# Window attention and a token/channel mixer on one core: the second half of a weight conversion put behind the split of x, and four edits to the first tiles

## The chip, the core and the metric

The kernel runs on one core of one Trainium2 chip. A core has five engines that each work through a queue of their own in program order and wait for each other by semaphores: PE multiplies matrices (its weight loads are listed apart, as PEld), DVE (VectorE) and ACT (ScalarE) do elementwise work, POOL (GpSimd) does elementwise work on SBUF alone, SP (SyncE) issues the DMA transfers. PE writes its results to PSUM, which this kernel lays out as eight banks of 128 x 512 f32 (`s`, `pt` and `h` two each, `av` and `up` one each); DVE and ACT read them from there.

The metric is the time of one execution on the device in microseconds (us). Three runs of the kernel before took 844.10, 844.76 and 845.11 us; the median is 844.76 us.

## The reference, cut to what matters

```
# q, k, v: (8, 8, 576, 64) f32; batch 8, 8 heads, 576 positions, 64 wide
scores = q @ k.T / sqrt(64);  mask = (0 <= i - j) & (i - j < 64)     # the last 64 positions
attn   = softmax(where(mask, scores, -1e9)) @ v
x      = attn, heads side by side: (8, 576, 512)
h = relu(x.T @ w_tok1) @ w_tok2                 # over positions: 576 -> 256 -> 576
u = x + h.T
h2 = relu(u @ w_ch1) @ w_ch2                    # over channels: 512 -> 1536 -> 512
out = u + h2                                    # f32
```

The four weight matrices come as 64-bit floats. The kernel gets their words as integers and turns them into f32 itself.

## The kernel before, in words

**Three stages.** The first, up to about 262 us of the profiled execution, is attention with the token mixer and most of the weight conversion. The second and third are the channel mixer: first three chunks of 512 tokens with plain products, while the weights are rewritten for a scheme of seven products per 2 x 2 block, then six chunks with that scheme. The change touches the first stage alone.

**Tiles.** Attention is cut into 36 tiles (`i` = 0 to 35), nine for each pair of batches. A tile holds two blocks of 64 query rows, one under the other in the 128 partitions, and all eight heads. Each block needs 128 keys. The tiles with `i % 9 == 4` hold the last block of both batches of a pair, and their x is split half by half (L345 to L349).

**Steps of one tile**, with the names that the profile shows:

- `qk` (L260): 32 small products give the scores `s`, in two PSUM banks (`u` = 0 and 1). In the first seven tiles (`N_PE`) the mask is first put into the bank by a product of `identr` and `maskr` (L270), and in the later ones DVE adds it.
- `softmax` (L280): the first seven tiles take the maximum from the bank (`nm`, L290, L291). Later ones scale and mask on DVE (`e`, L293) and take the maximum from there (`nm`, L296).
- `softmax_exp` (L298): eight exponentials on ACT, four for each bank, with their sums.
- `pt_transpose` (L307): PE transposes e into `pp` (L311), ACT copies it to `pt` (L313).
- `av` (L318): 32 products of pt and v give `xp` (L323). `recip` makes `ri` of the sums (L331, L332), `norm` multiplies: `x` = xp times ri (L337), on DVE.
- `split_x` (L342): ACT rounds x to `xhi` (L101), POOL takes the rest `xlo` (L104). With both, products in the fast format keep the precision.
- `tok1` (L439, products `h` at L368), `finish_h` (`hhi` on ACT, `hlo` on DVE, L388), `tok2` (a piece: transposes of x into a bank `up` at L409, six products at L416, a copy `u` on ACT at L421) are the token mixer. Pieces run one after the exponentials of the first bank and one at the end of a tile. All use one bank, so each waits for the copy of the one before.

**Conversion.** 28 jobs turn 320 or 384 columns of 64-bit weights into f32 during this stage, one each in most tiles (table `JOBS`: tiles up to 5, 12, and from 7 on those with `i % 9` other than 0, 3 and 5). A job has three parts:

- the first half, `job_convert_a`: three tensor_scalar operations `c` on DVE (L195, L197, L198);
- the second half, `job_convert_b`: `c` (L207), `r` (L209), `r` (L210) on DVE, then the sum `w` on POOL (L212);
- the finish, `job_finish`: ACT rounds w to `t1hi`, `t2hi` or `w1hi` (L101); the rest, `t1lo` or `w1lo`, is taken by POOL and `t2lo` by DVE (both L104). Jobs 0 to 3 make t1, 4 to 6 make t2, 7 to 22 make w1, the others go to memory.

**What sets the order.** Nothing is scheduled by a planner: each engine's queue is the order in which the loop at L478 writes the steps. Iteration `i` does the transposes and the product with v of tile i, the softmax of tile i + 1 and the scores of tile i + 2. On DVE an iteration is: maximum of the first bank, ri, the first half of a job, maximum of the second bank, the second half of the job, x of tile i, then hlo where a batch is finished. The first three tiles put their x into the next iteration (`N_EARLY`, L499, L535). The finish of a job stands ahead of the exponentials of the next iteration, but in iterations 4 and 5 behind them (L503, L526). `tok1_plan` (L472) says in which iteration tok1 takes which tile. Before, iteration 4 takes tiles 2 and 3, and iteration 5 takes tile 4.

The loads at the start are written out (L458 to L471), all on SP's queue.

Of the kernel before, what the change touches and what calls it, by code (L numbers as in the profile page):

```python
# [10 lines left out]
F32 = mybir.dt.float32  # L11
# [11 lines left out]
P = 128  # L23
# [22 lines left out]
TOK1_FROM, TOK1_SLOW, TOK2_FROM = 2, 4, 7  # L46

N_PE, N_EARLY = 7, 4

# [34 lines left out]
def mixer_kernel(ctx: ExitStack, tc: tile.TileContext, qh, kh, vh, wt1, wt2, wc1, wc2, out):  # L84
# [38 lines left out]
    with ExitStack() as actx:  # L123
# [28 lines left out]
        swapped = pa.tile([P, P], F32, name="swapped")  # L152
        make_identity(nc, ident)
        nc.scalar.copy(identr, ident)
        for m in (1, 0):
# [66 lines left out]
        def job_load():  # L222
            if to_load:
                n = to_load.pop(0)
                src, _, _, o, m = jobs[n]
                raw = cpool[0].tile([P, CW], I64, name=f"raw{n}", tag="raw", bufs=3)
                nc.sync.dma_start(raw[:, :m], src[:, o:o + m])
                to_convert.append((n, raw))
# [15 lines left out]
        def job_finish():  # L244
            if to_finish:
                n, w = to_finish.pop(0)
                finished.add(n)
                src, hi, lo, o, m = jobs[n]
                if hi is None:
                    nc.sync.dma_start(w2_dram[:, o:o + m], w)  # L250
                else:
                    eng = nc.vector if src is wt2 or n >= N_FIRST else nc.gpsimd
                    split(nc.scalar, eng, hi[:, o:o + m], lo[:, o:o + m], w)
                    if src is wt1 and o + m == 5 * DT:
                        for c, r in enumerate((top, bottom)):
                            nc.gpsimd.tensor_copy(t1z[r, c], t1lo[r, 4 * DT:].bitcast(F32))
# [3 lines left out]
        def qk(i):  # L260

            qt, on_pe = loaded[i][0], i < N_PE
            s = []
            for u in range(2):
                tag, bufs = ("up", 1) if on_pe and (2 * i + u) % 3 == 2 else ("s", 2)
                s.append(ps.tile([P, 4, P], F32, name=f"s{i}_{u}", tag=tag, bufs=bufs))
                s_ps[i, u] = s[u]
                if on_pe:
                    mk = maskr[1 if tile_blocks(i)[0][1] == 0 else 0]
                    nc.tensor.matmul(s[u], identr, mk.unsqueeze(1).to_broadcast([P, 4, P]), start=True, stop=False,  # L270
                                     skip_group_check=True)
            for j in range(4):
                for u in range(2):
                    r = slice(u * BLK, (u + 1) * BLK)
                    for half, (b, n) in enumerate(tile_blocks(i)):
                        nc.tensor.matmul(s[u][half * BLK:(half + 1) * BLK, j], qt[r, j, half],  # L276
                                         kbs[b][r, j, n * BLK:n * BLK + P],
                                         start=not on_pe, stop=True, skip_group_check=on_pe)
# [184 lines left out]
        job_load()  # L463
        load_q(1)
        load_v(0)
        for g in range(2):
            nc.sync.dma_start(k0[:, :, g, P:], kh0[:, :, g, P:])
        nc.sync.dma_start(kbs[0][:, :, 8 * BLK:], kh[0, :, :, 8 * BLK:])
        load_q(2)
        job_load()  # L470
# [7 lines left out]
        for i in range(-1, NT + 1):  # L478
# [44 lines left out]
                    job_convert_a()  # L523
            if i < N_PE - 1:
                softmax_exp(i + 1, 1)
                while to_finish:  # L526
                    job_finish()
# [4 lines left out]
            for _ in range(n_jobs):  # L532
                job_convert_b()
            if 0 <= i < NT:
                xp = av(i, pts)  # L535
                if i + 1 < N_EARLY:
# [6 lines left out]
            for n in tok1_plan.get(i + 1, ()):  # L543
                if n not in xhl:
                    split_x(n)
            run_pieces(min(have, n_pieces[1]))
            while to_load and len(to_convert) < 2 and i < NT - 2:
                job_load()
# [404 lines left out]
```

## Time and profile before

The profiled execution took 845.16 us, 0.40 us more than the median of the three runs. Its span, from the first instruction to the last, is 843.4 us; the other 1.76 us lie around it.

| | busy in the span | share |
|---|---|---|
| PE | 816.6 us | 97% |
| PEld | 678.4 us | 80% |
| DVE | 528.9 us | 63% |
| ACT | 336.8 us | 40% |
| POOL | 104.8 us | 12% |

The shares are means over stages that are unlike each other. In the stretch from 62 to 262 us DVE is busy for 178.45 us of 200, ACT for 166.63; after it DVE is busy for half of the time. PE's share hides the opposite: nearly all of its idle time lies in the first stage. A wait listed for an engine costs time only where that engine is late for the one that ends last, so the rows of PE are read first.

### The profile page before, as it was taken

To read this page: it belongs to the slowest core of one execution; us is meant where nothing else is said; L and a number is where in the kernel's file an instruction comes from. 1 tells how busy PE (TensorE), PEld (TensorE's weight loads), DVE (VectorE), ACT (ScalarE), POOL (GpSimd) and SP (SyncE) were. 2 spreads that over 40 slices of the span, in tenths; PEclk is the share of its full clock that TensorE was granted. 3 is DMA by queue.
4 is the path that set the end of the run, shared out by engine and by line. 5 is a ranking of instruction groups with operands and counts; after the bars stand their busy time and mean duration, and the time that the engine had idled before them with its cause. 6 is when DMAs were issued, how large, how long until landed. Compare 5 with 4: busy or idle time off the path is not lost.

```text
span 843.4 us, 14803 instructions
## 1 busy us (share of the span) xinstructions
PE 816.6 (97%) x5864; PEld 678.4 (80%) x5864; DVE 528.9 (63%) x939; ACT 336.8 (40%) x1017; POOL 104.8 (12%) x110
## 2 busy tenths in 40 slices
PE   6889999999999999999999999999999999999998
PEld 4668888888879878888888888888888878888886
DVE  4979988888884696566425535366635367625252
ACT  4778889898885341223203211124202033202020
POOL 3533444343332000000000000000000000000000
PEclk9999999999999999999999999999999999999999
DMA  9657687676644545745412652424542325542002
GB/s 320 218 184 245 209 249 255 216 256 235 220 134 151 166 149 166 225 128 149 131 82 93 245 211 87 138 88 137 187 187 88 137 88 167 169 176 88 1 0 100
DMA packets 71621, 136.49 MB, mean 162 GB/s; under 512 B 7040, under 2 KB 41856, under 8 KB 69632
## 3 DMA queue, kind: packets, MB, share of 16 engines
q1 hardware_dynamic: 69440, 133.71, 47.0%
q10 hardware_dynamic: 2112, 1.84, 0.7%
q8 instruction: 46, 0.75, 0.4%
q14 instruction: 23, 0.19, 0.1%
HBM read 104.66 MB, written 30.87 MB: 161 GB/s over the span
## 4 chain that ended last, share of the span: by engine, by line
PE 69%; DVE 23%; ACT 3%; issue 3%; DMA 1%; POOLq 0%; SPq 0%; POOL 0%; DVEq 0%; ACTq 0%
PE gp L852 18%; PE op L640 11%; PE gp L632 8%; PE op_4a L640 4%; PE op_2b L640 4%; PE op_2a L640 4%; PE op_0b L640 4%; PE op_0a L640 4%; PE op_4b L640 4%; DVE nm L296 3%; DVE e L293 2%; PE up L416 2%; DVE x L337 2%; PE h L368 2%; DVE r L210 2%
## 5 line engine op out<-in xcount | busy, mean ns | idle before, releaser
L852 PE MATMUL gp<-m,w1hi 128*128 128x512 f32 x504 | 155.4, 390 | 0.7 <-DVE x L860 0.7
L852 PEld LDWEIGHTS gp<-m,w1hi 128*128 128x128 f32 x504 | 94.5, 188 | 21.1 <-DVE x L860 1.5
L852 PE MATMUL gp<-m,w1lo 128*128 128x512 f32 x252 | 98.0, 389 | 0.0
L304 ACT ACTIVATE e<-e,nm 128x128 f32<-128x128 f32 x232 | 90.6, 398 | 18.2 <-DVE nm L296 17.6
L619 ACT ACTIVATE ghi<-x 128x512 fp32r<-128x512 f32 x54 | 34.1, 632 | 119.9 <-DVE x L862 68.2
L856 ACT COPY x<-gp 128x512 f32<-128x512 f32 x18 | 10.4, 579 | 143.3 <-PE gp L852 143.3
L620 DVE SCALAR_TENSOR_TENSOR glo<-x,ghi 128x512 fp32r<-128x512 f32 x54 | 37.4, 693 | 38.1 <-ACT ghi L619 38.1
L619 ACT ACTIVATE ghi<-gp 128x512 fp32r<-128x512 f32 x50 | 29.9, 597 | 69.6 <-PE gp L632 69.6
L632 PE MATMUL gp<-ulo,w1hi 128*128 128x512 f32 x144 | 56.0, 389 | 0.0
L632 PE MATMUL gp<-uhi,w1hi 128*128 128x512 f32 x144 | 56.0, 389 | 0.0
L632 PE MATMUL gp<-uhi,w1lo 128*128 128x512 f32 x144 | 56.0, 389 | 0.0
L852 PEld LDWEIGHTS gp<-m,w1lo 128*128 128x128 f32 x252 | 47.3, 188 | 9.9
L620 DVE SCALAR_TENSOR_TENSOR glo<-gp,ghi 128x512 fp32r<-128x512 f32 x50 | 34.4, 688 | 25.3 <-ACT ghi L619 25.2
L640 PE MATMUL op<-glo,w2hi 128*128 128x512 f32 x128 | 49.8, 389 | 0.0
L640 PE MATMUL op<-ghi,w2hi 128*128 128x512 f32 x128 | 49.8, 389 | 0.0
L640 PE MATMUL op<-ghi,w2lo 128*128 128x512 f32 x128 | 49.8, 389 | 0.0
L323 PEld LDWEIGHTS xp<-v,pt 128*64 128x64 f32 x1152 | 37.4, 140 | 14.1 <-issue 6.5
L104 POOL TENSOR_TENSOR xlo<-x,xhi 128x512 fp32r<-128x512 f32 x32 | 41.3, 1290 | 40.3 <-ACT xhi L101 39.9
L304 ACT ACTIVATION_READ_ACCUMULATOR e<-e,nm 128x1 f32 x232 | 45.1, 194 | 0.0
L276 PE MATMUL s<-k,q 64*64 64x128 f32 x1152 | 43.0, 284 | 1.2 <-DMA k<-kh 1.2
L323 PE MATMUL xp<-v,pt 128*64 128x64 f32 x1152 | 42.3, 227 | 1.1 <-ACT pt L313 0.8
L416 PE MATMUL up<-t2hi,hhi 128*128 128x320 f32 (+1 forms) x128 | 43.0, 336 | 0.0
(165 smaller groups left out, 1881.8 us busy)
## 6 DMA issues: line engine op xcount, KB each, us to landing
v<-vh SPq DMA_DIRECT2D x36, 512.0 KB, 3.9
w1hi<-w1s SPq DMA_DIRECT2D x18, 896.0 KB, 4.8
w1lo<-w1s SPq DMA_DIRECT2D x18, 896.0 KB, 6.5
raw<-wc SPq DMA_DIRECT2D x32, 384.0 KB, 4.4
q<-qh SPq DMA_DIRECT2D x36, 256.0 KB, 4.5
k<-kh SPq DMA_DIRECT2D x7, 1280.0 KB, 8.0
out<-uf SPq DMA_DIRECT2D x35, 256.0 KB, 2.7
uf<-u_dram SPq DMA_DIRECT2D x8, 1024.0 KB, 9.5
```

Source lines behind the costliest of these rows:

```text
L104: eng_lo.tensor_sub(lo, src, hi.bitcast(F32))
L210: nc.vector.scalar_tensor_tensor(out=rf, in0=low.bitcast(U32), scalar=2.0 ** -52, in1=rf, op0=ALU.mult, op1=ALU.mult)
L276: nc.tensor.matmul(s[u][half * BLK:(half + 1) * BLK, j], qt[r, j, half], kbs[b][r, j, n * BLK:n * BLK + P], start=not on_pe, stop=True, sk ...
L296: nc.vector.tensor_reduce(out=nmu, in_=e, axis=AX.X, op=ALU.max, negate=True)
L304: nc.scalar.activation(e[:, h], src[:, h], AF.Exp, bias=nm[:, g:g + 1], scale=by, accum_out=sm[:, g:g + 1])
L323: nc.tensor.matmul(xp[half * BLK:(half + 1) * BLK, h], pts[h % 2][:, h // 2, half * BLK:(half + 1) * BLK], vt[:, half, h], start=True, sto ...
L416: nc.tensor.matmul(up[:, :n], hx[:, cs], w[:, tt * S + s0:tt * S + s0 + n], start=False, stop=(k == 6), skip_group_check=True)
L619: nc.scalar.activation(hi, src, AF.Relu)
L620: nc.vector.scalar_tensor_tensor(out=lo, in0=src, scalar=0.0, in1=hi.bitcast(F32), op0=ALU.max, op1=ALU.subtract)
L632: nc.tensor.matmul(gp, w[:, w1_at(ft, ct)], x[:, ct], start=(k == 0), stop=(k == 3 * NCT - 1))
L640: nc.tensor.matmul(op, w[:, ct, ft], x[:, cols], start=(first and k == 0), stop=(last and k == 3 * len(gs) - 1), skip_group_check=not (fir ...
L852: nc.tensor.matmul(b, w[:, at], c[:, h, t], start=(n < 4 and k == 0), stop=(k == 5), skip_group_check=True)
```

## The change

Five edits, all in the first stage.

1. **Second half of a conversion.** From iteration 4 on, `job_convert_b` stands behind av, norm, hlo, the scores of tile i + 2 and the split of x, where it stood ahead of av. The finishes that iterations 4 and 5 have at their own place move along with it. In iterations below 4 the second half stays where it was.
2. **Plan of tok1.** `TOK1_SLOW` is 5: iteration 4 takes tile 2 alone, iteration 5 takes tiles 3 and 4. From iteration 6 on the plan is the same.
3. **Products of zeros.** DVE sets a tile of 128 x 256 f32 to zero at the start, and PE multiplies it with itself, four times ahead of the first mask and three times between the masks of tile 0 and its scores. Nothing reads the result.
4. **Banks of the scores.** Tile 1 uses the two banks `h`, which are free until tok1 starts. Tiles 2 to 6 use the bank `up` at another place in their turn, and the second half of tile 7 uses it too.
5. **Loads.** q of tile 1 and the rest of the first eight blocks of k go ahead of the first weights and of v of tile 0.

```
--- before.py
+++ after.py
@@ -43,7 +43,7 @@
 JOBS = {i: 1 if i < 6 or i == 12 or i > 6 and i % TPP not in (0, 3, 5) else 0 for i in range(-1, 37)}
 PIECES = {22: (1, 0), 23: (1, 0), 31: (1, 0), 32: (1, 0), 33: (1, 0), 34: (1, 0), 35: (3, 0), 36: (2, 1)}
 
-TOK1_FROM, TOK1_SLOW, TOK2_FROM = 2, 4, 7
+TOK1_FROM, TOK1_SLOW, TOK2_FROM = 2, 5, 7
 
 N_PE, N_EARLY = 7, 4
 
@@ -150,6 +150,15 @@
         maskr = [pa.tile([P, P], F32R, name=f"maskr{m}") for m in range(2)]
         identr = pa.tile([P, P], F32R, name="identr")
         swapped = pa.tile([P, P], F32, name="swapped")
+
+        zero = pa.tile([P, 256], F32, name="zero")
+        nc.vector.memset(zero, 0.0)
+        idle = ps.tile([P, 256], F32, name="idle", tag="av", bufs=1)
+
+        def warm(k):
+            for _ in range(k):
+                nc.tensor.matmul(idle, zero[:, :P], zero, start=True, stop=True)
+
         make_identity(nc, ident)
         nc.scalar.copy(identr, ident)
         for m in (1, 0):
@@ -262,13 +271,23 @@
             qt, on_pe = loaded[i][0], i < N_PE
             s = []
             for u in range(2):
-                tag, bufs = ("up", 1) if on_pe and (2 * i + u) % 3 == 2 else ("s", 2)
+
+                if i == 1:
+                    tag, bufs = "h", 2
+                elif (i, u) == (N_PE, 1) or 2 <= i < N_PE and (2 * i + u) % 3 == 0:
+                    tag, bufs = "up", 1
+                else:
+                    tag, bufs = "s", 2
                 s.append(ps.tile([P, 4, P], F32, name=f"s{i}_{u}", tag=tag, bufs=bufs))
                 s_ps[i, u] = s[u]
+                if i == 0 and u == 0:
+                    warm(4)
                 if on_pe:
                     mk = maskr[1 if tile_blocks(i)[0][1] == 0 else 0]
                     nc.tensor.matmul(s[u], identr, mk.unsqueeze(1).to_broadcast([P, 4, P]), start=True, stop=False,
                                      skip_group_check=True)
+            if i == 0:
+                warm(3)
             for j in range(4):
                 for u in range(2):
                     r = slice(u * BLK, (u + 1) * BLK)
@@ -460,11 +479,11 @@
         k0, kh0 = (x[:, :, :8 * BLK].rearrange("p j (g n) -> p j g n", g=2) for x in (kbs[0], kh[0]))
         for g in range(2):
             nc.sync.dma_start(k0[:, :, g, :P], kh0[:, :, g, :P])
-        job_load()
         load_q(1)
-        load_v(0)
         for g in range(2):
             nc.sync.dma_start(k0[:, :, g, P:], kh0[:, :, g, P:])
+        job_load()
+        load_v(0)
         nc.sync.dma_start(kbs[0][:, :, 8 * BLK:], kh[0, :, :, 8 * BLK:])
         load_q(2)
         job_load()
@@ -523,14 +542,13 @@
                     job_convert_a()
             if i < N_PE - 1:
                 softmax_exp(i + 1, 1)
-                while to_finish:
-                    job_finish()
             for n in tok1_plan.get(i, ()):
                 tok1(n)
             if N_PE - 1 <= i < NT - 1:
                 softmax_exp(i + 1, 1)
-            for _ in range(n_jobs):
-                job_convert_b()
+            if i < 4:
+                for _ in range(n_jobs):
+                    job_convert_b()
             if 0 <= i < NT:
                 xp = av(i, pts)
                 if i + 1 < N_EARLY:
@@ -543,6 +561,12 @@
             for n in tok1_plan.get(i + 1, ()):
                 if n not in xhl:
                     split_x(n)
+            if i >= 4:
+                if i < N_PE - 1:
+                    while to_finish:
+                        job_finish()
+                for _ in range(n_jobs):
+                    job_convert_b()
             run_pieces(min(have, n_pieces[1]))
             while to_load and len(to_convert) < 2 and i < NT - 2:
                 job_load()
```

**How it moves the instructions.** The first place is SP's queue at the start. It issues the loads of q, k, v and of the first weights (raw0) in this order before:

```order
L142 DMA q0_139<-qh 128x512
L462 DMA k0_138<-kh 128x4x128 x2
L227 DMA raw0_143<-wt1 128x320
L142 DMA q1_145<-qh 128x512
L147 DMA v0_147<-vh 128x1024
L467 DMA k0_138<-kh 128x4x128 x2
L468 DMA k0_138<-kh 128x4x128
```

and in this order with the change:

```order
L142 DMA q0_142<-qh 128x512
L481 DMA k0_141<-kh 128x4x128 x2
L142 DMA q1_146<-qh 128x512
L484 DMA k0_141<-kh 128x4x128 x2
L236 DMA raw0_150<-wt1 128x320
L147 DMA v0_152<-vh 128x1024
L487 DMA k0_141<-kh 128x4x128
```

Three issues, q1 and two of k, now stand ahead of raw0, and two of k ahead of v0.

The second place is DVE's queue around x of tile 24, in a run of three tiles with jobs (19 and 20 are the jobs, L207 to L210 the second half). Before:

```order
L296 TENSOR_REDUCE nm25_2946<-e25_1_2973 128x4
L207 SCALAR_TENSOR_TENSOR c19_2969<-raw19_2600,c19_2969 128x384
L209 TENSOR_SCALAR r19_2992<-c19_2969 128x384
L210 SCALAR_TENSOR_TENSOR r19_2992<-raw19_2600,r19_2992 128x384
L337 TENSOR_TENSOR x24_3015<-xp24_2998,ri24_2951 128x512
L293 SCALAR_TENSOR_TENSOR e26_0_3071<-s26_0_3017,mask0_90 128x512
L296 TENSOR_REDUCE nm26_3069<-e26_0_3071 128x4
L331 TENSOR_SCALAR ri25_3074<-sum25_2947 128x8
```

With the change (L356 is the line of x, L216 to L219 are the second half):

```order
L315 TENSOR_REDUCE nm25_2956<-e25_1_2983 128x4
L356 TENSOR_TENSOR x24_3019<-xp24_3002,ri24_2961 128x512
L216 SCALAR_TENSOR_TENSOR c19_2979<-raw19_2610,c19_2979 128x384
L218 TENSOR_SCALAR r19_3043<-c19_2979 128x384
L219 SCALAR_TENSOR_TENSOR r19_3043<-raw19_2610,r19_3043 128x384
L312 SCALAR_TENSOR_TENSOR e26_0_3081<-s26_0_3021,mask0_90 128x512
L315 TENSOR_REDUCE nm26_3079<-e26_0_3081 128x4
L350 TENSOR_SCALAR ri25_3084<-sum25_2957 128x8
```

x and the second half change places; the scaling of the next tile (e26_0) still follows both.

The third place is POOL's queue in the same tiles. Before:

```order
L104 TENSOR_TENSOR xlo24_3036<-x24_3015,xhi24_3035 128x512
L104 TENSOR_TENSOR w1lo_67<-w19_2993,w1hi_66 128x384
L212 TENSOR_TENSOR w20_3111<-r20_3110,c20_3093 128x384
L104 TENSOR_TENSOR xlo25_3154<-x25_3133,xhi25_3153 128x512
L104 TENSOR_TENSOR w1lo_67<-w20_3111,w1hi_66 128x384
```

With the change:

```order
L221 TENSOR_TENSOR w19_3044<-r19_3043,c19_2979 128x384
L104 TENSOR_TENSOR w1lo_67<-w19_3044,w1hi_66 128x384
L104 TENSOR_TENSOR xlo25_3158<-x25_3137,xhi25_3157 128x512
L221 TENSOR_TENSOR w20_3162<-r20_3161,c20_3103 128x384
L104 TENSOR_TENSOR w1lo_67<-w20_3162,w1hi_66 128x384
```

The order per job was w, xlo, w1lo and is now xlo, w, w1lo.

More of the change, by code (lines that the diff above doesn't have):

```diff
@@ L152, in mixer_kernel, with warm @@
         swapped = pa.tile([P, P], F32, name="swapped")
+        zero = pa.tile([P, 256], F32, name="zero")
+        nc.vector.memset(zero, 0.0)
+        idle = ps.tile([P, 256], F32, name="idle", tag="av", bufs=1)
+        def warm(k):
+            for _ in range(k):
+                nc.tensor.matmul(idle, zero[:, :P], zero, start=True, stop=True)
         make_identity(nc, ident)
@@ L264, in qk @@
             for u in range(2):
-                tag, bufs = ("up", 1) if on_pe and (2 * i + u) % 3 == 2 else ("s", 2)
+                if i == 1:
+                    tag, bufs = "h", 2
+                elif (i, u) == (N_PE, 1) or 2 <= i < N_PE and (2 * i + u) % 3 == 0:
+                    tag, bufs = "up", 1
+                else:
+                    tag, bufs = "s", 2
                 s.append(ps.tile([P, 4, P], F32, name=f"s{i}_{u}", tag=tag, bufs=bufs))
                 s_ps[i, u] = s[u]
+                if i == 0 and u == 0:
+                    warm(4)
                 if on_pe:
@@ L531, in mixer_kernel @@
                 softmax_exp(i + 1, 1)
-            for _ in range(n_jobs):
-                job_convert_b()
+            if i < 4:
+                for _ in range(n_jobs):
+                    job_convert_b()
             if 0 <= i < NT:
@@ L545, in mixer_kernel @@
                     split_x(n)
+            if i >= 4:
+                if i < N_PE - 1:
+                    while to_finish:
+                        job_finish()
+                for _ in range(n_jobs):
+                    job_convert_b()
             run_pieces(min(have, n_pieces[1]))
```

10 lines of the change are left out of this document (5 added, 5 removed).

## The prediction

> **What bounds the kernel now.** First the page's chain of waits, then the busy time by stage.
>
> ```profile
> PE 69%; DVE 23%; ACT 3%; issue 3%; DMA 1%; POOLq 0%; SPq 0%; POOL 0%; DVEq 0%; ACTq 0%
> ```
> ```profile
> 0.00:62.00 62.00, 47.43 (x630) 34.82 (x631) 45.24 (x102) 41.18 (x163) 24.23 (x40) 0.97 0.70 240
> 62.00:262.00 200.00, 193.39 (x2665) 166.35 (x2663) 178.45 (x336) 166.63 (x621) 80.29 (x70) 1.00 0.66 219
> 262.00:843.40 581.40, 575.74 (x2573) 477.18 (x2572) 305.24 (x502) 129.03 (x234) 0.23 (x1) 1.00 0.39 134
> ```
>
> The columns are the stretch, its length, then PE, PEld, DVE, ACT and POOL busy. The chain gives DVE 23%, some 194 us, but PE is idle for only 14.6 us before 62, 6.6 us from there to 262 and 5.7 us after. PE and DVE are both nearly full in the attention, so the chain may follow either. PE's work stays the same, bar the zeros; what the change can win is those first two idle shares, 21 us at most. PE's longest wait from 62 to 262 says who causes most of the second one (total, times, longest):
>
> ```profile
> PE up L409 <- ACT u L421: 4.9, 7, 1.1
> ```
>
> DVE has little room either, and part of its busy time is standing. The groups of that stretch and some rows of its timeline:
>
> ```profile
> L331 DVE TENSOR_SCALAR ri<-sum 128x8 f32<-128x8 f32 x29 | 21.4, 736 | 0.0
> L197 DVE TENSOR_SCALAR c<-c 128x384 f32<-128x384 f32 x21 | 12.4, 588 | 0.7
> L198 DVE TENSOR_SCALAR c<-c 128x384 int32<-128x384 int32 x21 | 9.7, 460 | 0.7
> ```
> ```profile
> 180.23 0.16 DVE L331 TENSOR_SCALAR ri<-sum 128x8 f32<-128x8 f32 x1
> 180.55 1.25 DVE L195 TENSOR_SCALAR c<-raw 128x384 int32<-128x384 int32 x1
> 181.83 0.36 DVE L197 TENSOR_SCALAR c<-c 128x384 f32<-128x384 f32 x1
> ...
> 180.28 1.30 POOL L104 TENSOR_TENSOR xlo<-x,xhi 128x512 fp32r<-128x512 f32 x1 [3.37 <-ACT xhi L101]
> ```
>
> L195, started 0.27 us behind POOL's xlo, ends 0.22 us behind xlo's end (181.58); ri takes 0.16 us and L197 0.36 us where POOL rests, and L198 has L197's shape. So a tensor_scalar on DVE stands until POOL's operation is done. By the groups this costs 29 x (736 - 160) ns = 16.7 us at ri, 21 x (588 - 360) = 4.8 at L197 and 21 x (460 - 360) = 2.1 at L198. So the question of edit 1 is which of POOL's operations meet which of DVE's.
>
> **Start: loads, zeros, banks.**
>
> ```profile
> 2.57 0.62 SPq L227 DMA_DIRECT2D raw<-wt  x1
> 4.18 1.62 SPq L467 DMA_DIRECT2D k<-kh  x2
> 6.56 1.98 PE L276 MATMUL s<-k,q 64*64 64x128 f32 x30 [0.95 <-DMA k<-kh]
> 10.16 0.32 DVE L195 TENSOR_SCALAR c<-raw 128x320 int32<-128x320 int32 x1
> 11.12 0.79 PE L270 MATMUL s<-maskr,identr 128*128 128x512 f32 x1 [1.85 <-ACT e L304]
> 12.13 0.49 DVE L210 SCALAR_TENSOR_TENSOR r<-raw,r 128x320 f32<-128x320 uint32 x1
> 12.31 1.58 PEld L276 LDWEIGHTS s<-k,q 64*64 64x64 f32 x30 [0.19 <-DMA k<-kh]
> 14.32 0.69 DVE L290 TENSOR_REDUCE nm<-s 128x4 f32<-128x512 f32 x1 [1.70 <-PE s L276]
> 19.82 0.69 DVE L290 TENSOR_REDUCE nm<-s 128x4 f32<-128x512 f32 x1 [0.42 <-PE s L276]
> ```
>
> DVE waits at 14.32 for tile 1's scores, which wait for a bank (11.12) and for k (12.31). Now the bank is free and k goes ahead. Sizes by the shapes: 768 KB were needed at 6.56 and 2368 KB at 12.31, so 3.6 us per 1000 KB. q1 and k stand at 1536 KB, about 9.3 us; scores at the slow 2.4 us end by 11.8. raw0 stands at 1856 KB, 10.5 us. Job 0 takes DVE 2.46 us (10.16 to 12.62), so nm(1) starts at 12.9 instead of 14.32, and the 0.42 at 19.82 goes too: **1.8 us**. Bounds: 2.1 if raw0 is there at 10.16 as before, 0.1 if it takes as long from its issue as 2.57 to 10.16 (then 12.2). v of tile 0 now stands at 2368 KB, 12.3 us; its first use is behind tile 1's scores, tile 0's transposes and two ACT copies, so it is not late. The zeros hide under the wait for k that ends at 6.56. Their price is not shown; the nearest rows are the plain f32 products at 6.56, 66 ns for 128 columns on a quarter of the array. For 256 columns that is 0.13 us each if these ran one by one, 0.53 if four ran side by side: 0.9 to 3.7 us for seven. I take the upper end, for the matrix here is four times as large. From DVE's zero at about 1 us, four end near 3.1, the masks (1.22 us before) near 4.7, three near 6.3: under the wait for k, nothing. Anything beyond delays the scores one for one. Scores at a faster clock than the 1.98 us are worth nothing either: nm of tile 0 is done by 10.2 as it is, and DVE then waits for raw0 at 10.5.
>
> **Tiles 4 and 5.**
>
> ```profile
> 44.37 0.56 DVE L104 TENSOR_TENSOR t2lo<-w,t2hi 128x384 fp32r<-128x384 f32 x1 [1.79 <-ACT t2hi L101]
> 49.35 1.33 DVE L197 TENSOR_SCALAR c<-c 128x384 f32<-128x384 f32 x1
> 52.73 0.56 DVE L104 TENSOR_TENSOR t2lo<-w,t2hi 128x384 fp32r<-128x384 f32 x1 [1.66 <-ACT t2hi L101]
> 56.46 0.68 DVE L293 SCALAR_TENSOR_TENSOR e<-s,mask 128x512 f32<-128x512 f32 x1
> ```
>
> On the way to e of tile 7, at 56.46, DVE stands for 1.79 + 1.66 us behind t2hi, and for 0.97 us of L197's 1.33: 4.4 us. With the finish behind x and its split, the first t2lo waits for xhi, xlo and t2hi on ACT, about 1.8 again; the second for 0.7, since hlo (1.2 us) covers ACT's xhi; the meeting at 49.35 goes, as xlo of tile 4 is done a tile half earlier, with 0.3 for another. That leaves 2.8: **1.4 us** won after rounding down. Bounds: 0 if the waits only change their names, 3.4 if both t2lo waits vanish. Queued behind each t2lo on DVE is the second half and then the next maximum, on which ACT's exponentials wait. The plan of tok1 takes six products out of PE's wait for x of tile 3 and costs nothing elsewhere, as PE idles in tile 5. The other banks cost nothing: `h` is free until tok1 starts, and the first piece that wants `up` comes an iteration after DVE has read tile 7 from it. In tiles 3 to 6 the second bank still waits for exponentials of the same iteration, as before.
>
> **Edit 1 in the full tiles.** A tile in a run with jobs:
>
> ```profile
> 187.26 0.81 DVE L331 TENSOR_SCALAR ri<-sum 128x8 f32<-128x8 f32 x1
> 188.60 1.21 POOL L104 TENSOR_TENSOR w1lo<-w,w1hi 128x384 fp32r<-128x384 f32 x1 [0.55 <-ACT w1hi L101]
> 188.97 1.05 DVE L198 TENSOR_SCALAR c<-c 128x384 int32<-128x384 int32 x1
> 189.63 1.15 PE L323 MATMUL xp<-v,pt 128*64 128x64 f32 x32
> 190.66 0.69 DVE L296 TENSOR_REDUCE nm<-e 128x4 f32<-128x512 f32 x1
> 191.44 0.40 ACT L304 ACTIVATE e<-e,nm 128x128 f32<-128x128 f32 x1 [1.12 <-DVE nm L296]
> 192.79 0.68 DVE L337 TENSOR_TENSOR x<-xp,ri 128x512 f32<-128x512 f32 x1
> 192.95 1.01 POOL L212 TENSOR_TENSOR w<-r,c 128x384 f32<-128x384 f32 x1 [3.14 <-DVE r L210]
> 193.51 0.62 ACT L101 CAST xhi<-x 128x512 fp32r<-128x512 f32 x1 [0.41 <-DVE x L337]
> 194.20 1.29 POOL L104 TENSOR_TENSOR xlo<-x,xhi 128x512 fp32r<-128x512 f32 x1 [0.24 <-ACT xhi L101]
> 194.45 0.55 PE L409 MATMUL up<-ident,x 128*128 128x128 f32 x3 [0.67 <-ACT u L421]
> ```
>
> *Gain.* PE's 0.67 waits for u, u for xhi, xhi for x, x for the second half. Let X be the end of nm, 191.35. x now runs at X, and xhi follows the four exponentials (to X + 1.65) instead of x at X + 2.1, so u is some 0.5 to 0.6 us earlier. Over the seven gaps (4.9 us) that is up to 3.9; I take **3.0** (0 to 4.9), since a later DVE takes some back.
>
> *Cost.* xlo runs from X + 2.4 to 3.7 and now w comes right behind, to X + 4.8; w1hi and w1lo follow w. On DVE ri is due at X + 3.45 and stands 0.3 (was 0.65). L195 then meets w, 0.8 new. L198 may meet w1lo as before, 0.7: counted from w's end, it is due at 0.22 + 0.03 + 0.39 = 0.64, and w1lo after ACT's w1hi (0.53) and two hand-overs, 0.6 to 0.7. A tile costs 1.1 or 1.8; before, 0.65 or 1.35, and by the groups about 1.2 in the ten tiles that follow a job tile and have a w1lo. At even odds 0.2 each, **+2.0** (bounds -1 and +6). Third, x now waits for xp where PE is the later one, and the second half behind it waits too. Tile 10 shows it:
>
> ```profile
> 86.12 0.69 DVE L296 TENSOR_REDUCE nm<-e 128x4 f32<-128x512 f32 x1
> ...
> 86.31 1.15 PE L323 MATMUL xp<-v,pt 128*64 128x64 f32 x32
> ```
>
> nm ends at 86.81, xp at 87.46: 0.65 us that the second half (1.5 us) covered. In a full run it is the other way round (xp, 1.15 us from 189.63, ends at 190.78; X is 191.35). Nine job tiles begin a run: 0 to 5.9 us. DVE, being late, closes the gap itself, so I take **+1.0**. Behind 262 nothing moves.
>
> The page "SBUF — State Buffer" of the Trainium skill (section "Who interferes with whom") says that whoever of the two engines starts first holds a port pair for its whole instruction; the rows at 180.55 agree. It adds that a DVE operation with two SBUF inputs meets a reading GpSimd operation as well. L207 and L210 are such, and no row of this trace has them beside POOL.
>
> **Sum.** -1.8 - 1.4 - 3.0 + 2.0 + 1.0 = -3.2 us: the profiled 845.16 becomes 842.0, and 0.40 lower against the median of the runs, **841.6 us**.
>
> **Rivals.**
>
> - *Slower: w1lo wins.* It is ahead of L198 at 0.64 us from w's end in every tile: +5.6, the wait for xp 1.8, nothing won at u, the start's -3.2: +4.2, 849.0 us. For it: in the rows at 188.60 and 188.97 a w1lo that arrives under L197 goes ahead of L198. Against: the two are level by the rows. Chance 0.20.
> - *No change.* raw0 is as late as its issue (0.1 won), tiles 4 and 5 keep their waits, and 3.0 against 3.0 in the full tiles: 844.7 us. For it: DMAs in the first 12 us land together. Chance 0.22.
> - *More: both shares.* L198 always wins (-1.5 in place of +2.0), all seven gaps close (4.9), no wait for xp, capped by PE's 6.6 idle at about 5; with 3.2 from the start 836.6 us. Chance 0.15.
> - *The second half meets xlo.* Where x waits for xp by about 1.5 us, as in the lone job tiles 22 and 31, xlo starts under L207 to L210. If L210 stands for xlo's 1.29 us in two such tiles, the sum is -0.6: 844.2 us. For it: L210 reads two tensors of SBUF, as POOL's operation does. Against: nothing shows that such operations stand. Chance 0.05. By the Trainium skill's rule on two inputs (same page and section) it would come.
>
> **Numbers.** The forecast has 0.38, with 840 to 843 as its own range. The bound for a difference that a measurement of this kernel can tell is 0.2%, 1.7 us. Faster: 0.38 and 0.15, 0.53; same: the second and fourth rival with little else, 0.25; slower: 0.22. The range of 837 to 848 leaves out about half of the first rival and half of the third.
>
> **What would show it.** nm(1) near 12.9 us and the first L195 near 10.5; e of tile 7 near 53.3 instead of 56.46; from there PE's wait for u under 2 us; ri near 0.45 us mean, L195 near 0.8; L198's mean tells the first rival (0.8) from the third (0.36). If DVE's busy time from the tile at 60 us on grows by more than 5 us, or PE's idle time after 62 us rises, the sum is wrong at edit 1.

## The result

The changed kernel takes 859.67 us (median of 4 runs, 859.09 to 861.05), the kernel before 844.73: a ratio of 1.0183, with a 95% interval of 1.0171 to 1.0195. It is 15 us slower. The forecast was 841.6 us with a range up to 848, so it was wrong in sign and in size.

The profiled execution of the changed kernel has a span of 857.3 us, 13.9 us more than before. The stretch from x of tile 6 to the first product of the channel mixer holds all of it, and more (same columns as in the prediction's table by stage; first the kernel before, then the changed one):

```profile
59.97:273.31 213.34, 206.65 (x2786) 178.87 (x2787) 184.27 (x344) 175.30 (x644) 80.53 (x70) 1.00 0.66 217
```
```profile
57.60:287.73 230.13, 216.19 (x2752) 182.67 (x2751) 189.84 (x345) 174.53 (x644) 81.64 (x70) 0.99 0.60 200
```

It starts 2.4 us earlier and lasts 16.8 us longer. PE's idle time there goes from 6.7 to 13.9 us. Its busy time grows by 9.5 us, though the work is the same. A part of that is the clock: in the changed kernel the granted clock is 0.63 from 60 to 64 us, 0.68 from 280 to 284 and 0.89 from 284 to 288, together 3.2 us less than a full clock gives, where before it is full in the whole stretch. The rest is put down here to short gaps, which can count as busy since the ends of products are modelled. The waits of the weight loads show more of them. Of before, and of the changed kernel, from 58 to 290 us (total, times, longest):

```profile
PEld up L409 <- ACT u L421: 7.4, 10, 1.4
...
PEld pp L311 <- ACT e L304: 2.0, 9, 0.3
```
```profile
PEld up L428 <- ACT u L440: 10.4, 16, 2.3
PEld pp L330 <- ACT e L323: 7.7, 22, 1.5
PEld s L295 <- DVE e L312: 5.2, 10, 0.8
```

PE now waits for exponentials (7.7 us, was 2.0) and for score banks that DVE has not read yet (5.2 us; no such row before). ACT's waits from 58 to 275 us say why the exponentials are late. Before, and in the changed kernel:

```profile
ACT e L304 <- DVE nm L296: 17.6, 17, 1.4
ACT xhi L101 <- DVE x L337: 7.4, 18, 0.5
```
```profile
ACT e L323 <- DVE nm L315: 18.8, 21, 1.5
ACT w1hi L101 <- POOL w L221: 16.9, 16, 2.4
ACT xhi L101 <- DVE x L356: 4.0, 4, 3.1
```

The second row of the changed kernel is new: w1hi waits for w in each of its 16 jobs, 16.9 us in all. One tile's rows, first of before, then of the changed kernel:

```profile
159.31 1.00 POOL L212 TENSOR_TENSOR w<-r,c 128x384 f32<-128x384 f32 x1 [3.53 <-DVE r L210]
...
160.46 0.69 DVE L296 TENSOR_REDUCE nm<-e 128x4 f32<-128x512 f32 x1
...
160.56 1.29 POOL L104 TENSOR_TENSOR xlo<-x,xhi 128x512 fp32r<-128x512 f32 x1 [0.25 <-ACT xhi L101]
...
161.60 0.53 ACT L101 CAST w1hi<-w 128x384 fp32r<-128x384 f32 x1
162.02 0.42 ACT L304 ACTIVATE e<-e,nm 128x128 f32<-128x128 f32 x1
```
```profile
166.13 1.28 POOL L104 TENSOR_TENSOR xlo<-x,xhi 128x512 fp32r<-128x512 f32 x1 [3.88 <-ACT xhi L101]
...
166.55 0.69 DVE L315 TENSOR_REDUCE nm<-e 128x4 f32<-128x512 f32 x1
...
167.37 1.02 POOL L221 TENSOR_TENSOR w<-r,c 128x384 f32<-128x384 f32 x1
...
168.42 0.51 ACT L101 CAST w1hi<-w 128x384 fp32r<-128x384 f32 x1 [1.14 <-POOL w L221]
168.84 0.40 ACT L323 ACTIVATE e<-e,nm 128x128 f32<-128x128 f32 x1
```

Before, w ended at 160.31, 1.3 us ahead of w1hi, and the first exponential started 0.87 us behind the end of its maximum. Now w stands behind xlo on POOL and ends at 168.39, ACT waits 1.14 us for it, and the exponential starts 1.60 us behind its maximum.

DVE changes too. Its groups from 58 to 275 us answer to those of L331, L195, L197, L198 and L210 before (736, 353, 588, 460 and 559 ns):

```profile
L356 DVE TENSOR_TENSOR x<-xp,ri 128x512 f32<-128x512 f32 x30 | 20.6, 686 | 17.6 <-PE xp L342 17.6
L219 DVE SCALAR_TENSOR_TENSOR r<-raw,r 128x384 f32<-128x384 uint32 x21 | 16.6, 790 | 0.7
L204 DVE TENSOR_SCALAR c<-raw 128x384 int32<-128x384 int32 x21 | 14.9, 708 | 0.0
L207 DVE TENSOR_SCALAR c<-c 128x384 int32<-128x384 int32 x21 | 14.3, 682 | 0.7
L206 DVE TENSOR_SCALAR c<-c 128x384 f32<-128x384 f32 x21 | 11.9, 567 | 0.7
...
L350 DVE TENSOR_SCALAR ri<-sum 128x8 f32<-128x8 f32 x29 | 9.9, 341 | 0.0
```

Beyond the times that these operations take alone (0.16 us for ri, 0.32, 0.36 and 0.36 for the first half, 0.56 for L219) DVE stands 5.2 us at ri, 8.1 at L204, 4.3 at L206, 6.8 at L207 and 4.8 at L219: 29.3 us, where it was 24.3. The three parts of this move apart: ri stands 11.5 us less, the first half 11.7 us more, and the 4.8 us at L219 are new. And x waits 17.6 us for xp, where it was 10.9.

So three causes are there to be told apart: the new wait in ACT's queue, DVE's standing beside POOL, and the second half's place on DVE ahead of the next tile's maxima, which makes x wait for xp (the "ring": x, maxima, exponentials, transposes, xp, x). Below they are the queue theory, the collision theory and the ring theory. The first runs were made with the last two in mind alone.

### The profile page after: what moved, and what is told of

Same layout as the page of the kernel before. It is cut to its first block, busy times and chain, and to the rows that moved or that the text cites. A ratio compares the mean times of both kernels' runs of the same rounds, so it can differ in the third digit from the quotient of the medians.

```text
span 857.3 us, 14827 instructions
## 1 busy us (share of the span) xinstructions
PE 830.8 (97%) x5878; PEld 686.4 (80%) x5878; DVE 535.8 (62%) x940; ACT 336.0 (39%) x1017; POOL 106.0 (12%) x110
## 4 chain that ended last, share of the span: by engine, by line
PE 68%; DVE 20%; ACT 5%; issue 3%; POOL 2%; DMA 1%; POOLq 0%; SPq 0%; DVEq 0%; ACTq 0%
PE gp L876 18%; PE op L664 11%; PE gp L656 8%; PE op_4a L664 4%; PE op_2b L664 4%; PE op_2a L664 4%; PE op_0a L664 4%; PE op_0b L664 4%; PE op_4b L664 4%; ACT e L323 3%; DVE r L219 2%; PE h L387 2%; PE up L435 2%; DVE e L312 2%; DVE nm L315 2%
## 5 line engine op out<-in xcount | busy, mean ns | idle before, releaser
L295 PE MATMUL s<-k,q 64*64 64x128 f32 x1152 | 45.5, 278 | 5.6 <-DVE e L312 2.8
L330 PE MATMUL pp<-ident,e 128*128 128x128 f32 x288 | 45.4, 285 | 3.9 <-ACT e L323 2.8
```

Source lines behind the costliest of these rows:

```text
L330: nc.tensor.transpose(pp[:, h], e[:, h], ident)
```

## The experiments

Each stands beside 844.6 to 844.9 us of the kernel before on the same chip. Intervals are of the ratio to it, at 95%; 0.1% is 0.8 us.

**Which edit.** The change without edit 1, and edit 1 alone.

```
start_alone, from the changed kernel:
-            if i < 4:
-                for _ in range(n_jobs):
-                    job_convert_b()
+            for _ in range(n_jobs):
+                job_convert_b()
...
-            if i >= 4:
-                if i < N_PE - 1:
-                    while to_finish:
-                        job_finish()
-                for _ in range(n_jobs):
-                    job_convert_b()
```

In start_alone the finishes of iterations 4 and 5 go back to their old place as well; move_alone is the kernel before with the hunks of the loop alone.

> The change without its first edit: the second half stands ahead of x in every tile, as before; zeros, banks, loads and the plan of tok1 are those of the change. Ring theory (the second half now lies on the ring x, next maxima, exponentials, transposes, xp, x, where before it lay beside DVE's wait for xp) and collision theory (POOL's xlo, w and w1lo meet more of DVE's operations) agree here: x of tile 8 comes 2.4 us earlier in the changed kernel than before, so this one should take about 842 us (841 to 843.5). If the start's edits themselves cost (the changed kernel's x of tile 6 lost 3.8 us of the 6.2 that it was ahead at tile 5), 845 or more.

> The kernel before with the first edit alone: second half (and the finishes of tiles 4 and 5) behind the split of x from tile 4 on; loads, banks, plan and clock as before. Ring and collision theory: the whole loss comes from here, 860 to 863 us. If the start's edits are a part of the loss, under 858.

start_alone took 841.75 us (0.9954 to 0.9979), move_alone 862.75 (1.0197 to 1.0228). Edits 2 to 5 win 3.0 us, and edit 1 costs 17.9 us on top of them and 18.0 alone: the whole loss is edit 1's, as both theories had it.

**POOL's order without DVE's.** DVE's three operations stay ahead of x, and w alone is issued behind xlo, from tile 4 on (`job_add` issues what is on the list).

```
-            (nc.vector if late else nc.gpsimd).tensor_add(w, rf, cf)
+            if late:
+                nc.vector.tensor_add(w, rf, cf)
+            else:
+                to_add.append((w, rf, cf))
...
                     split_x(n)
+            job_add()
```

> Start's edits, DVE's order as before (the second half's three operations ahead of x), but POOL's w issued behind xlo from tile 4 on, as in the changed kernel: POOL's order of the change with DVE's order of before. Ring theory: as start_alone or within 3 us of it (842 to 845), and x keeps its place. Collision theory: xlo, w and w1lo run back to back beside ri and the first half as in the changed kernel, so most of the 13 us of tiles 8 to 35 come back: 851 to 858.

861.16 us (1.0180 to 1.0210). It loses 19.4 us against start_alone though DVE's order is that of before: w's place on POOL is enough for the whole loss, without the ring, and even the collision theory had not asked for so much. Its standing grows most in this kernel's group of L204, and ACT has the same wait as in the changed kernel:

```profile
L204 DVE TENSOR_SCALAR c<-raw 128x384 int32<-128x384 int32 x21 | 19.9, 949 | 0.0
```
```profile
ACT w1hi L101 <- POOL w L231: 17.5, 16, 2.2
```

**Fewer tiles moved.** The second half stays ahead of x in the job tiles whose next tile has none.

```
-            if i < 4:
+            ahead = i < 4 or i >= N_PE and not JOBS.get(i + 1)
+            if ahead:
```

> The changed kernel, but in the job tiles whose next tile has no job (9 of the 21 from tile 7 on) the second half stays ahead of x. Ring theory: the tiles without a job, which lost 1.0 us each in the changed kernel (5.6 to 6.6 us, 7.6 us in the eight of them), lose nothing: 851 to 852.5. Collision theory: the loss goes with the number of tiles moved, 12 of 21: about 854 (853 to 856), and a tile without a job still lasts more than 5.9 us.

851.74 us (1.0065 to 1.0095), where the ring theory put it. Read alone it would have settled the matter wrongly: ACT's wait for w, which neither theory knew, falls with the tiles too, to 10 waits.

```profile
ACT w1hi L101 <- POOL w L221: 8.4, 10, 1.1
```

**The same tile, two places.** The second half of the last job of each run goes into the tile without a job behind it, once ahead of that tile's maxima (moved_at_ends) and once behind them, ahead of x (spread).

```
moved_at_ends, from start_alone:
-            for _ in range(n_jobs):
-                job_convert_b()
+            behind = i >= N_PE and not JOBS.get(i + 1)
+            if not behind:
+                for _ in range(n_jobs):
+                    job_convert_b()
...
                     split_x(n)
+            if behind:
+                for _ in range(n_jobs):
+                    job_convert_b()

spread, from start_alone:
-            for _ in range(n_jobs):
-                job_convert_b()
+            if i < N_PE or not n_jobs or JOBS.get(i + 1) or i >= NT - 1:
+                while to_convert_b:
+                    job_convert_b()
```

> start_alone with the second half behind the split of x only in those job tiles whose next tile has no job (from tile 7 on): the eight second halves between two tiles of the attention then lie in the tile without a job, ahead of its maxima. Ring theory: such a tile gets 1.0 us longer, as in the changed kernel (5.6 to 6.6 us), its wait for xp stays at 1.5 us, and the job tile ahead of it gets shorter by up to 1.5 us: 838 to 842 us. Collision theory: no first half follows in these tiles, so nothing new is met: the 1.5 us of every job tile are won, 832 to 836.

> start_alone with the second half of the same job tiles (those whose next tile has no job, from tile 7 on) held over to the tile without a job as well, but at the old place there: behind the maxima, ahead of x, where DVE waits 1.4 to 1.8 us for xp. Ring theory: the wait is filled, the tile stays under 5.9 us and the job tile ahead of it gets shorter by up to 1.5 us, until PE is full (6.6 us idle in 62 to 262 before): 833 to 837 us, at least 3 us faster than moved_at_ends. Collision theory: as moved_at_ends within 1.5 us, as the same operations lie in the same tiles beside the same ones of POOL.

moved_at_ends took 850.49 us (1.0054 to 1.0082), spread 839.21 (0.9926 to 0.9951). The place is worth 11.3 us, but both theories missed moved_at_ends, and spread is 2 us above the range of the ring theory, which was wrong on how spread wins: the tile without a job still lasts 6.6 us there and x still waits up to 1.6 us for xp, as PE has little idle time left (it waits 2.6 us for u in all). The gain over start_alone lies in the job tile ahead, 5.9 us where it was 7.5. In moved_at_ends w lies behind xlo, and ACT waits for it again; behind five of the six waits the next tile lasts 0.9 to 2.0 us longer than in spread, where there is no such row:

```profile
ACT w1hi L101 <- POOL w L221: 7.2, 6, 2.4
```

**Without w.** POOL's w is left out from job 7 on in both.

```
-            nc.vector.scalar_tensor_tensor(out=rf, ...)
-            (nc.vector if late else nc.gpsimd).tensor_add(w, rf, cf)
+            nc.vector.scalar_tensor_tensor(out=w if left_out else rf, ...)
+            if not left_out:
+                (nc.vector if late else nc.gpsimd).tensor_add(w, rf, cf)
```

> start_alone with POOL's w left out from job 7 on: the third operation of the second half writes what was r into w's buffer, so the low word is not added and the weights' values are not the reference's. POOL then has xlo and w1lo alone. It is the base for after_no_w. w met none of the first half's operations in start_alone, so 840 to 842 us by either theory.

> The changed kernel with POOL's w left out from job 7 on, as in start_no_w. Without w, nothing of POOL's lies behind xlo in the tile, and the change takes ri out from beside xlo (5.2 us of standing in tiles 8 to 35, not 15.6); its first half meets w1lo as in start_no_w. So DVE stands no longer than in start_no_w. Collision theory: then the loss of 17.9 us is gone, 840 to 845 us. Ring theory (the second half ahead of the next tile's maxima makes e and the exponentials late, for which PE's scores and transposes wait): 9 to 14 us over start_no_w remain, 850 to 855 us.

start_no_w took 843.63 us (0.9974 to 0.9993), 1.9 more than start_alone, which no theory here explains. after_no_w took 846.89 (1.0012 to 1.0031), 1.9 us above what the collision theory allowed and 3 below the other. Against its base the loss is 3.3 us, not 17.9: 14.6 us hang on w. But w's absence takes away three things at once: DVE's standing beside it, the delay of w1lo, and ACT's wait.

**ACT's wait.** The finish of a job (w1hi on ACT, then w1lo on POOL) goes behind the first four exponentials. Nothing else moves on ACT, and DVE's order stays.

```
-            if i not in (4, 5):
+            if i < N_PE and i not in (4, 5):
                 while to_finish:
                     job_finish()
 ...
                 softmax_exp(i + 1, 0)
+            if i >= N_PE:
+                while to_finish:
+                    job_finish()
```

> The changed kernel with the finish of a job (w1hi on ACT, then w1lo on POOL) behind the first four exponentials of the next tile instead of ahead of them, from tile 7 on. DVE's order is that of the change, POOL's xlo and w too. Queue theory (the loss comes from the exponentials that stand behind w1hi, which waits for w, which now waits for xlo): 16.9 us of waiting go, 845 to 850 us, near after_no_w's 846.9. Collision theory (DVE stands beside w and w1lo): the standing of the first half beside w stays, 855 to 860. Ring theory: 857 to 860.

> w_behind_xlo (861.16 us; DVE's order of before, w behind xlo on POOL) with the finish of a job behind the first four exponentials. Queue theory: w1hi's wait of 17.5 us goes, 843 to 849 us. Collision theory: its 35.5 us of standing in tiles 8 to 35 (23.4 in start_alone) stay for the most part, 855 to 861 us.

> start_alone (841.75 us) with the finish of a job behind the first four exponentials: the base for the two above. w1hi waits for nothing there (0.1 us), so by the queue theory the place is worth little: the exponentials come 0.5 us earlier in a job tile, w1lo later: 840 to 843 us by every theory.

| | finish ahead of the exponentials | behind them | won |
|---|---|---|---|
| changed kernel | 859.67 | 849.59 (1.0030 to 1.0066) | 10.1 |
| w behind xlo, DVE as before | 861.16 | 847.22 (1.0019 to 1.0039) | 13.9 |
| start_alone | 841.75 | 840.47 (0.9934 to 0.9965) | 1.3 |

The queue theory's ranges hold all three, the other theories' only the base. The wait's row is gone from after_hi_late, and so is PE's row of score banks; the longest of ACT's and DVE's waits that are left there:

```profile
ACT e L323 <- DVE nm L315: 16.8, 20, 1.5
ACT u L440 <- PE up L435: 6.8, 11, 1.0
ACT e L323 <- DVE ri L350: 5.7, 5, 1.5
```
```profile
DVE x L356 <- PE xp L342: 19.7, 16, 2.1
```

But w1lo moves along with w1hi, and DVE's standing falls too. Over the whole execution DVE is busy for 535.8 us in the changed kernel and for 526.6 in after_hi_late; with w behind xlo it is 543.4 and 532.5. The collision theory's ranges rested on a standing that stays, so missing them does not rule it out, and how the 10.1 us are shared between ACT's wait and DVE's standing stays open. moved_at_ends points to a cost of ACT's wait by itself: it loses 8.7 us to start_alone with DVE no busier (529.5 and 529.3 us), and ACT waits 7.2 us there. Of the loss 3.4 us go with a lower granted clock (0.57 from 180 to 184 and from 272 to 276 us); the 5.3 us left are more than the whole loss of after_no_w, where more tiles are moved. w_behind_hi_late points to a cost of DVE's standing by itself: with ACT's wait for w down to 0.6 us and DVE's order that of before, it loses 6.8 us to start_hi_late, with DVE busy for 5.8 us more (532.5 and 526.7).

after_hi_late still takes 9.1 us more than start_hi_late, and x waits 19.7 us for xp where start_alone has 10.9. In after_no_w that wait is 20.5 us, at a loss of 3.3. More standing of DVE cannot be the cause in after_hi_late, as DVE is busy just as long in start_hi_late; PE is busy 7.7 us longer at the same work. First after_hi_late, then start_hi_late:

```profile
PE 827.0 (97%) x5878; PEld 686.5 (81%) x5878; DVE 526.6 (62%) x940; ACT 337.0 (40%) x1017; POOL 105.3 (12%) x110
```
```profile
PE 819.3 (98%) x5878; PEld 680.4 (81%) x5878; DVE 526.7 (63%) x940; ACT 336.3 (40%) x1017; POOL 104.7 (12%) x110
```

Most of these 7.7 us go with the clock. In after_hi_late the granted clock is 0.57 from 60 to 64, from 180 to 184 and from 272 to 276 us, together 5.2 us less than a full clock gives; in start_hi_late it is full from 28 us on. The runs of after_hi_late point the same way: three at a mean clock of 0.990 took 849.2 to 850.0 us, one at 0.994 took 847.5. after_no_w has 3.4 us of it behind 60 us, as much as its loss, and start_no_w none. So what the new order on DVE and its wait for xp cost shows for the most part as a lower clock. Ahead of the fall at 180 us PE stood for 1.3 us until 178.1, waiting for exponentials; that such a wait brings the fall about was not tried.

**Terms of the start.** Loads and banks alone; start_alone with the old plan of tok1 (so with the zeros); and the changed kernel with the move in tiles 4 to 6 only.

```
start_old_plan, from start_alone:
-TOK1_FROM, TOK1_SLOW, TOK2_FROM = 2, 5, 7
+TOK1_FROM, TOK1_SLOW, TOK2_FROM = 2, 4, 7

moved_4_5, from the changed kernel:
-            if i < 4:
+            if not 4 <= i < N_PE:
...
-            if i >= 4:
+            if 4 <= i < N_PE:
```

loads_banks is the kernel before with the hunks of the change on the banks (without the products of zeros) and on the loads.

> The kernel before with the other loads and the other banks of the scores alone: no products of zeros, the old plan of tok1, the old place of the second half. The prediction gave the loads and banks 1.8 us and the zeros and the plan nothing: 843.0 us. If the zeros (whose first scores took 1.10 us instead of 1.98) carry a part of start_alone's 3.0 us, it is 843.5 to 844.5; if loads and banks carry all of it, 841.7.

> start_alone with the old plan of tok1 (TOK1_SLOW 4): beside loads_banks (842.96 us) it has the products of zeros, beside start_alone (841.75 us) it lacks the plan. If the zeros carry the 1.2 us between them, it is 841.7; if the plan does (six products out of PE's wait in tile 3), 843.0. The prediction gave both nothing.

> The changed kernel with the second half (and the finishes) moved in tiles 4 to 6 alone; from tile 7 on it stays ahead of x. Beside start_alone (841.75 us) it prices the move in these tiles. The prediction's term is -1.4 us, which gives 840.4; by the ring theory there is nothing to win, since x of tile 7 in the changed kernel had lost about 0.9 us against start_alone, as far as one execution of each tells: 842 to 843.

loads_banks took 842.96 us (0.9971 to 0.9991), start_old_plan 843.05 (0.9972 to 0.9991), moved_4_5 843.48 (0.9975 to 0.9993). Loads and banks win 1.8 us, the zeros nothing that shows, the plan 1.3, and the move in tiles 4 to 6 costs about 1.7, so that the run is slower than either expectation had it. The last two differences are at the edge of what the intervals tell apart.

**A faster kernel.** Every second half is held over to the next tile's old place, behind its maxima (hold_all), and then the finish goes behind the exponentials as above (hold_hi_late).

```
-            for _ in range(n_jobs):
+            while len(to_convert_b) > (n_jobs if N_PE <= i < NT - 1 else 0):
                 job_convert_b()
```

> start_alone with every second half from tile 7 on held over to the next tile's old place (behind its maxima, ahead of x), not only the last of a run as in spread. The work is shared out as in spread, one operation group in the tiles without a job, but the light tile is the first of a run, not the last. Ring theory: nothing lies ahead of the maxima, so as spread within 2 us, 837 to 841 us. Collision theory: w and w1lo come a tile later beside the same operations, so as spread as well; what it tells is whether there is more to win than spread's 839.2 us.

> hold_all (838.89 us) with the finish of a job behind the first four exponentials. By the queue theory nothing is waited for there, as w is done a tile half before: 837.5 to 840 us. If w1lo now meets more of the first half's operations, up to 843.

838.89 us (0.9912 to 0.9941) and 837.63 (0.9895 to 0.9927), both as expected. hold_hi_late has the lowest median here, 0.9% below the kernel before; the intervals do not tell it from hold_all. ACT does not wait for w in it, PE waits 0.9 us for u, and x waits 4.5 us for xp:

```profile
PE up L428 <- ACT u L440: 0.9, 2, 0.6
```
```profile
DVE x L356 <- PE xp L342: 4.5, 8, 1.2
```

## Why the prediction was wrong

**The term that is missing: what w's delay does on ACT.** The step "xlo runs from X + 2.4 to 3.7 and now w comes right behind, to X + 4.8; w1hi and w1lo follow w" was right on POOL (in the tile shown above, with X at 163.80, xlo runs from X + 2.3 to 3.6, and w to X + 4.6). It then priced only what DVE's operations meet. It did not ask where w1hi stands in ACT's queue, though the finish stands ahead of the next exponentials there. The prediction's own rows had the number. w1lo starts at 188.60 when w1hi ends, so w1hi (0.53 us) began near 188.05. The tile lasts about 7.45 us, so the X before was 191.35 - 7.45 = 183.90, and w1hi began near X + 4.1, with w due at X + 4.8: 0.65 us of waiting in 16 jobs, some 10 us. The sum has nothing for this. The trace has 16.9 us of waiting, and the runs that move w or w1hi give or take the loss with it: w behind xlo alone costs 19.4 us, and w1hi behind the exponentials wins 10.1 us, a part of which may be DVE's standing. No rival had this mechanism either.

**Gain, -3.0: not there.** PE's wait for u is 4.8 us from 62 to 275, where it was 4.9, in smaller pieces:

```profile
PE up L428 <- ACT u L440: 4.8, 13, 0.7
```

x did run earlier within the tile, but the tile itself got longer. With w left out the wait falls from 5.5 us (start_no_w) to 2.0 (after_no_w), so the mechanism is there and was overrun.

**Collisions, +2.0 (bounds -1 and +6): 5.0 us, inside the bounds by luck.** At ri and the first half, the operations that the step priced, DVE stands 24.5 us now and 24.3 before, so the step's own price is 0.2 us. ri fell to 0.34 us (0.45 foretold), and what that won L204 (0.71, 0.8 foretold) and L207 (0.68, nearer to the rival's 0.8 than to 0.36) took back. The growth is the 4.8 us at L219: five of its 21 operations take 1.52 to 1.55 us beside POOL's rest of x. That is the mechanism of the fourth rival, which had a chance of 0.05 and a price of 2.6 us (last section). The rival "w1lo wins", 849.0 us, lacked the missing term as well.

**x's wait for xp, +1.0 (bounds 0 and 5.9): mis-sized.** It grew by 6.7 us, above its bound. "DVE, being late, closes the gap itself" was wrong: a second half ahead of the maxima delays e, the exponentials and xp with it, so the wait comes back in the tile without a job. The bound of nine tiles counted only those that begin a run; the changed kernel has 16 such waits. Its price in time is 3.3 us in the runs without w. With the late finish 9.1 us are left, of which 5.2 us go with the clock; what lowers the clock stays open.

**Loads and banks, -1.8: right.** loads_banks measured -1.8. Tile 1's first maximum was foretold for 12.9 us; in the changed kernel and in start_alone, whose starts are the same, it came at

```profile
11.90 0.68 DVE L309 TENSOR_REDUCE nm<-s 128x4 f32<-128x512 f32 x1
```
```profile
13.16 0.69 DVE L309 TENSOR_REDUCE nm<-s 128x4 f32<-128x512 f32 x1
```

so one execution does not fix such a time to better than about 1 us. The zeros cost and win nothing that shows, as foretold, but by luck: they were to end near 6.3 us, under the wait for k, and end at 6.79 in the changed kernel. The first scores start there at 6.71, where loads_banks has 5.95, and take 1.10 us instead of 1.98, so that the two cancel. The plan of tok1, taken at nothing, won about 1.3, at the edge of the intervals.

**Tiles 4 and 5, -1.4: not won; about +1.7, its sign at the edge of the intervals.** In moved_4_5 e of tile 7 starts at 55.68, in start_alone at 54.86. The step counted the waits behind t2hi and left out what the second half itself delays: it now stands ahead of tile 6's first maximum, and it met POOL's xlo for more than 1 us. These are DVE's and POOL's rows of moved_4_5:

```profile
43.97 1.50 POOL L368 TENSOR_TENSOR xlo<-x,xlo 64x512 fp32r<-64x512 f32 x1
44.24 1.65 DVE L216 SCALAR_TENSOR_TENSOR c<-raw,c 128x384 int32<-128x384 int32 x1
```

t2hi waits for w in these tiles too, 3.0 us by ACT's waits from 38 to 66 us:

```profile
ACT t2hi L101 <- POOL w L221: 3.0, 1, 3.0
```

**What bounds the kernel.** The reading that PE and DVE are both nearly full was right, and it holds the lesson: the sum priced no wait on ACT, which was 83% busy in the same stretch. In the rows at 168.42 and 168.84 the exponential stands behind w1hi's wait in ACT's queue, and with 6.6 us of idle time on PE such waits reach it: its weight loads wait 7.7 us for exponentials, where it was 2.0.

## What to carry to other kernels

When a producer is moved behind another operation, follow its consumers by queue as well as by data: for each one, find when it used to start, and what stands behind it on its engine. Here a result that nobody needed for several us held up four exponentials that everything needed, and moving its consumer by a few places won 10.1 of the 17.9 us lost, a part of it perhaps because another operation on POOL moved along. When a loss is shared out, look at the granted clock of both runs too: here 5.2 of 9.1 us lay there. Work that only has to be done some time belongs behind the operations on which other engines wait, also when that is one tile later.

## What the runs showed of the hardware

A DVE operation with two inputs in SBUF does stand beside POOL's. L216 above takes 1.65 us from 44.24, where it takes 0.55 otherwise, and ends behind the xlo that started 0.27 us before it (43.97 to 45.47). Two rows of the changed kernel show the same beside POOL's rest of a split x with L219, 1.55 us instead of 0.56:

```profile
178.76 1.27 POOL L368 TENSOR_TENSOR xhi<-x,xhi 64x512 fp32r<-64x512 f32 x1 [4.33 <-ACT xhi L367]
178.90 1.55 DVE L219 SCALAR_TENSOR_TENSOR r<-raw,r 128x384 f32<-128x384 uint32 x1
```

The prediction knew this only as a rule of the Trainium skill ("SBUF — State Buffer", "Who interferes with whom": a DVE operation with two SBUF inputs contends with a GpSimd operation that reads SBUF) and gave it 0.05, since no row of the trace had the two side by side. These rows agree with it.

By the recorded starts, the first of two does not always hold the other off for its whole length. These rows of the changed kernel have a tensor_scalar that starts 0.04 us behind xlo and runs its normal 0.31 us, while xlo takes 1.50 us instead of 1.28; the next one stands until xlo is done:

```profile
172.93 1.50 POOL L104 TENSOR_TENSOR xlo<-x,xhi 128x512 fp32r<-128x512 f32 x1 [2.92 <-ACT xhi L101]
172.97 0.31 DVE L204 TENSOR_SCALAR c<-raw 128x384 int32<-128x384 int32 x1
173.32 1.33 DVE L206 TENSOR_SCALAR c<-c 128x384 f32<-128x384 f32 x1
```

POOL's spans are rough, so 0.04 us may not be the true order of the two; that xlo takes 0.22 us longer would fit L204 as the first.
